# Joining each weight piece one step later in a fused scan and gated feed-forward kernel

## Chip, core and metric

The kernel runs on one core of a Trainium2 chip. Its time is the device time of one execution in microseconds (us); before the change the median of three executions is 376.66 us (376.62 to 376.97). The profiled execution spans 374.1 us, and the profile grants TensorE its full clock all through it.

Names used below, as in the profile: PE is TensorE (matrix products), PEld its loading of weights, DVE is VectorE, ACT is ScalarE, POOL is GpSimd, SP is SyncE, which here only issues transfers. L668 is line 668 of the kernel before. "hp", "k", "w", "gT", "mag" and so on are the names of tiles.

## What is computed

Two blocks follow each other. The first is a chunked state-space scan over x, a, B, C (4 sequences, 8 heads, 768 positions, 32 features, state 16). Its result, seen as a matrix of 3072 rows and 256 columns, goes through a feed-forward block:

```
h = x @ w_in          # 3072 x 256 by 256 x 2048
g = h * cos(h)
out = g @ w_out       # 3072 x 2048 by 2048 x 256
```

The two weight matrices arrive as 64-bit floating-point numbers, while the kernel calculates in 32 bits. So the kernel rebuilds each weight from its two 32-bit words before TensorE can use it. That rebuilding is what the change moves.

## The kernel before, in words

**Tiling.** The sequence is cut into six chunks of 128 positions, and all four sequences of a chunk are done together (512 rows). Each chunk needs 16 feed-forward steps, so step n belongs to chunk n // 16, and there are 96 steps. In chunk 0 two neighbouring steps, 2i and 2i+1, use the same pair i of 128-column blocks of w_in and the matching two row blocks of w_out: step 2i for one half of the rows and step 2i+1 for the other. In the later chunks each half has its eight steps in a row.

**One step.** `first(n)` (L668) forms h on PE: eight matmuls of 128x256 in a PSUM tile hp. `wind_k(n)` (L675, ACT) rounds h over 2 pi to an integer k, `wind_w(n)` (L681, DVE) subtracts it, `gate(n)` (L690, ACT) takes the cosine by a sine, and `gated(n)` (L695, DVE) multiplies it with h and leaves gT in SBUF. `second(n)` adds the product with w_out two steps later (LAG is 2): L739 in chunk 0, L777 after it. The hp tiles of ordinary steps come from two PSUM banks in turn, so `first(n+2)` can start only when `gated(n)` has read its bank.

**Order.** The schedule is manual: every engine does its instructions in the order in which the program emits them. In the main loop PE is given `first(n)`, then `second(n-2)`, and then, at some steps, the products of the scan. DVE is given `wind_w(n)`, the join of a weight piece if the step has one, `gated(n)`, and then what the list `behind` holds: halves of the decay scan of the next chunk (`halved`, a DVE scan over arow at L515) and masked products (`masked`, L586).

**Weight pieces.** w_in and w_out are cut into eight pieces each, named ("in", 0) to ("in", 7) and ("out", 0) to ("out", 7). Piece i of either serves steps 2i and 2i+1 of chunk 0. Each is fetched as 128 x 512 pairs of words. Two stages rebuild it:

- `grade`: ACT takes the absolute value of the high word as a float (L231, to mag), POOL clips it (L232), and ACT converts the low word (L229, to last). With `later=True` the last of these is emitted separately, behind `gate`.
- `join`: DVE shifts the bits (L244) and puts in the sign and top bits from the high word (L246); POOL adds the low bits and writes the finished piece into w_in or w_out (L254).

The table `piece` names a piece for each step of chunk 0: ("out", n/2) for an even n and ("in", (n+3)/2) for an odd one. The loop at step n grades `piece[n + 1]` and joins `piece[n]`. The steps 0 to 3 are written out by hand in `first_steps`, which also grades and joins ("in", 3) and grades ("out", 2); the main loop begins at step 4 (AHEAD). Tiles mag and last have three buffers each, words has eight.

**Later users of the engines.** From step 14 on POOL forms sums and differences of w_out blocks (`differ_w`, L714), and from step 16 on those of gT (`differ`, L720 to L723), for the seven-product scheme (`seven`) that the later chunks use.

Of the kernel before, what the change touches and what calls it, by code (L numbers as in the profile page):

```python
# [25 lines left out]
def kernel(  # L26
# [168 lines left out]
    def kept(which, i):  # L195
        return (w_in[:, :, i * WC:(i + 1) * WC] if which == "in" else
                w_out[:, i * WF:(i + 1) * WF])
# [12 lines left out]
    held = {}  # L210

    def shares(which, ap, n):

        return [ap] if n == 1 else [ap.rearrange("p (k e f) -> p e k f", k=KT, e=n)[:, e]
                                    for e in range(n)]

    def grade(which, i, later=False, n=1):


        t = words.pop((which, i), None)  # L220
        if t is None:
            return
        mag = conv.tile([P, 2 * WC], FP32, tag="mag", bufs=3, name="mag")
        last = conv.tile([P, 2 * WC], U32, tag="last", bufs=3, name="last")
        low, high, mags, lasts = (shares(which, ap, n) for ap in (t[:, :, 0], t[:, :, 1], mag, last))
        held[which, i] = list(zip(high, shares(which, mag.bitcast(U32), n), lasts))

        def rest(e=0):
            ACT.activation(lasts[e], low[e], AF.Copy, scale=2.0 ** -29)  # L229
        for e in range(n):  # L230
            ACT.activation(mags[e], high[e].bitcast(FP32), AF.Abs)  # L231
            G.tensor_scalar(out=mags[e], in0=mags[e], scalar1=MOST, scalar2=LEAST,  # L232
                            op0=ALU.min, op1=ALU.max)
            if not later:
                rest(e)
        if later:
            return rest

    def join(which, i):


        parts = held.pop((which, i), ())
        for e, (high, bits, last) in enumerate(parts):
            V.tensor_scalar(out=bits, in0=bits, scalar1=3, scalar2=0x3FFFFFFF,  # L244
                            op0=ALU.logical_shift_left, op1=ALU.bitwise_and)
            V.scalar_tensor_tensor(out=bits, in0=high, scalar=0xC0000000, in1=bits,  # L246
                                   op0=ALU.bitwise_and, op1=ALU.bitwise_or)
            dst = kept(which, i)
            if len(parts) > 1:
                dst = dst[:, :, e * P:(e + 1) * P]  # L250
            else:
                bits, last = (ap.rearrange("p (k f) -> p k f", k=dst.shape[1])
                              for ap in (bits, last))
            G.tensor_tensor(out=dst.bitcast(U32), in0=bits, in1=last, op=ALU.add)  # L254
# [10 lines left out]
    for s in range(2):  # L265
# [3 lines left out]
        out=a_in, in_=a.rearrange("(u b) h (c p) -> (b h c) u p", u=NU, p=P))  # L269
# [96 lines left out]
    def weigh0(k):  # L366
        scs[k] = sc = scan.tile([P, 2 * H, N], FP32, tag="sc0", bufs=1, name="sc0")
        G.tensor_tensor(out=sc, in0=bs[:, k].rearrange("p q (h n) -> p (q h) n", h=H),
                        in1=lams[k].rearrange("p q h i -> p (q h) i")[:, :, W - 1:W]
                        .to_broadcast([P, 2 * H, N]), op=ALU.mult)  # L370
# [53 lines left out]
    def weights(k, q):  # L424

        m_of[k] = units[k]
        m, l = (ap[:, :, HH * q:HH * (q + 1)].rearrange("p s (k t) i -> p k s (t i)", k=2)
                for ap in (units[k], lams[k]))
        V.tensor_tensor(out=m, in0=gs[k, q][:, :, 0:2 * P].rearrange("p k (s i) -> p k s i", s=2),
                        in1=l, op=ALU.mult)  # L430
# [224 lines left out]
    def first(n, between=None, tag="h"):  # L655
        c, f = divmod(n, NF)
        hp[n] = bank([P, TB], "hp", tag) if tag else pair("hp")[:, 0]

        u, j = turn_of(n)
        if c == 0:  # L660
            to_, y = hp[n].rearrange("p (e i) -> p e i", e=2), yT[0][:, u]
        else:
            to_ = hp[n].rearrange("p (e t s i) -> p e t s i", e=2, t=2, s=2)
            y = yT[c].rearrange("p k (u s t i) -> p k u t s i", u=2, s=2, t=2)[:, :, u]
        for e in range(2):
            fs = slice((2 * j + e) * P, (2 * j + e + 1) * P)
            for k in range(KT):
                PE.matmul(to_[:, e], lhsT=w_in[:, k, fs], rhs=y[:, k],  # L668
                          start=(k == 0), stop=(k == KT - 1), skip_group_check=True)
            if between and e == 0:  # L670
                between()

    def wind_k(n):
        k = ffn.tile([P, TB], I32, tag="k", name="k")
        ACT.activation(k, hp[n], AF.Copy, bias=0.25, scale=INV_2PI)  # L675
        turns[n] = k
# [11 lines left out]
    def gate(n):  # L688
        cos = turns[n]
        ACT.activation(cos, cos, AF.Sin, bias=quarter, scale=TWO_PI)  # L690
# [181 lines left out]
    def units_of_decay():  # L872
        G.tensor_copy(out=unit[:, 0:HH * P].rearrange("p (h i) -> p h i", h=HH),
                      in_=ident.unsqueeze(1).to_broadcast([P, HH, P]))
        G.tensor_copy(out=unit[:, HH * P:], in_=ident[:, 0:W])
# [10 lines left out]
    piece = {n: ("in", (n + 3) // 2) if n % 2 else ("out", n // 2) for n in range(NF)}  # L886
# [47 lines left out]
    def first_steps():  # L934

        grade("in", 1)
        weigh0(1)
        units_of_decay()
        for q in range(2):
            weights(1, q)  # L940
        states_of = []
        first(0, lambda: states_of.extend(finish0(1)))
        take_s1, add_s1 = states_of
        join("in", 1)
        rests = [grade("out", 0, later=True)]
        wind_k(0)
        take_s1()
        rests.pop()()
        wind_w(0)
        first(1)  # L950
        join("out", 0)
        wind_k(1)
        gate(0)
        wind_w(1)
        gate(1)
        gated(0)
        gated(1)
        first(2, tag=None)
        rests = [grade("in", 2, later=True)]
        clips()  # L960
        wind_k(2)
        rests.append(grade("out", 1, later=True))
        rests.pop(0)()
        wind_w(2)
        join("in", 2)
        first(3, tag=None)
        gate(2)
        rests.pop()()
        join("out", 1)
        gated(2)  # L970
        second(0)
        wind(3)
        rest = grade("in", 3, later=True)
        gate(3)
        rest()
        second(1)
        join("in", 3)
        gated(3)
        grade("out", 2)
        return add_s1  # L980

    add_s1 = first_steps()
# [1 line left out]
    for n in range(AHEAD, NC * NF + LAG):  # L984
        c, f = divmod(n, NF)
        if n < NC * NF:

            if c > 0 and f == (NJ if c == 1 else 0):
                if c == 1:
                    load(2, only=(x,))  # L990
                load(c + 2)
            first(n)
            wind(n)
            for at in pairs(n):
                turn2(*at)
            rests = []
            if n + 1 in piece:
                rests.append(grade(*piece[n + 1], later=True))
            gate(n)
            for rest in rests:  # L1000
                if rest:
                    rest()
            if n in piece:
                join(*piece[n])

            behind = [lambda at=at: halved(*at) for at in halves_at(n)]
            behind = [lambda at=(c, 2 * u + 1): masked(*at) for c, u in pairs(n - 2)] + behind
            if n not in piece and behind:
                behind.pop(0)()
            gated(n)  # L1010
            if n == AHEAD + 2:
                add_s1()
            for do in (*behind, *unsummed):
                do()
            unsummed.clear()
        for i, js in differ_at.get(n, ()):
            differ_w(i, js)
        if n >= LAG:
            second(n - LAG)
        for c, u in pairs(n - 1):  # L1020
            intra2(c, u)
            masked(c, 2 * u)
        for c, us in ends(n):
            finish2(c, us)
            if 1 in us:
                raw.pop(c)
        for c, u in pairs(n + 1):
            for b in (2 * u, 2 * u + 1):
                reaches(c, b)
                load_along(c + 1, (b,))  # L1030
            if by_blocks(c, u):
                turn_blocks(c, u)
        for at, (c, u) in block_loads.items():
            if at == n:
                loading = load_blocks(c, u)
            if at <= n < at + 8:
                for _ in range(4):
                    next(loading)
# [30 lines left out]
```

## Time and profile before

| engine | busy, us | share of the span | instructions |
|---|---|---|---|
| PE | 364.3 | 97% | 3262 |
| DVE | 282.7 | 76% | 473 |
| POOL | 216.1 | 58% | 334 |
| ACT | 172.1 | 46% | 293 |

The shares are averages over stages. Chunk 0's steps of the main loop lie between about 27 and 80 us; there DVE is much busier than its average. A busy share of PE is not PE at its peak, because its matmuls overlap and their ends are modelled, so PE is best judged by its idle times and by the distance between the starts of neighbouring groups. The mean durations of the operations that the change moves, where nothing disturbs them: L231 0.67 us, L229 0.67 us (ACT), L232 0.61 us (POOL), L244 0.42 us and L246 0.69 us (DVE), L254 1.27 us (POOL). One half of the decay scan (L515, 128 x 512) takes 1.92 us in this stage.

### The profile page before, as it was taken

How to read it: one execution, taken by the hardware profiler on the slowest of the kernel's cores; microseconds unless marked ns; L12 is line 12 of the kernel's file. 1: busy time of each engine (PE TensorE's matmuls, PEld its weight loads, DVE VectorE, ACT ScalarE, POOL GpSimd, SP SyncE). 2: the span in 40 equal slices, each digit the busy share in tenths (PEclk: the TensorE clock that was granted, in tenths of full speed). 3: DMA queues.
4: the chain of work that ended last, by engine and by line, in shares of the span. 5: the costliest groups of instructions: out<-in, count | busy, mean ns of one | idle time of the engine just before them, and what ended most of it. 6: DMA issues, size and time to landing. Idle time of an engine off the chain costs nothing.

```text
span 374.1 us, 8667 instructions
## 1 busy us (share of the span) xinstructions
PE 364.3 (97%) x3262; PEld 326.9 (87%) x3262; DVE 282.7 (76%) x473; ACT 172.1 (46%) x293; POOL 216.1 (58%) x334
## 2 busy tenths in 40 slices
PE   8998999999999999999999999999999999999996
PEld 5687777889899899999899998999999989999995
DVE  7788999989699957987867987766887872554543
ACT  3586756444344434354434435434444443443442
POOL 6667765589946346665454693453785344544451
PEclk9999999999999999999999999999999999999999
DMA  9969797514545742653222745221020000010011
GB/s 147 283 180 257 206 255 127 128 14 97 140 106 76 133 95 31 88 151 93 59 54 22 133 99 135 28 45 17 3 41 8 13 18 2 2 28 0 2 31 29
DMA packets 121354, 31.55 MB, mean 84 GB/s; under 512 B 90496, under 2 KB 117216, under 8 KB 121312
## 3 DMA queue, kind: packets, MB, share of 16 engines
q1 hardware_dynamic: 119024, 30.54, 38.3%
q10 hardware_dynamic: 2288, 0.46, 0.7%
q8 instruction: 26, 0.43, 0.5%
q14 instruction: 16, 0.13, 0.1%
HBM read 27.64 MB, written 3.34 MB: 83 GB/s over the span
## 4 chain that ended last, share of the span: by engine, by line
PE 64%; DVE 13%; SPq 7%; POOL 7%; issue 4%; ACT 2%; DMA 2%; DVEq 0%; POOLq 0%; ACTq 0%
PE hp L668 30%; PE o L777 25%; SPq L155 4%; POOL words L714 3%; DVE gT L695 2%; DVE w L681 2%; PE y L607 2%; SPq L110 2%; DVE mag L246 2%; DVE lam L515 2%; DVE mag L244 2%; DMA arow<-a_cut 1%; PE y L600 1%; PE g L565 1%; PE a_ps L351 1%
## 5 line engine op out<-in xcount | busy, mean ns | idle before, releaser
L668 PE MATMUL hp<-yT,w_in 128*128 128x256 f32 x768 | 183.5, 382 | 3.2 <-DVE gT L695 2.9
L668 PEld LDWEIGHTS hp<-yT,w_in 128*128 128x128 f32 x768 | 139.3, 190 | 23.8 <-issue 5.7
L720 POOL TENSOR_TENSOR gd<-gT 128x256 f32<-128x256 f32 x79 | 59.0, 747 | 99.1 <-DVE gT L695 97.2
L690 ACT ACTIVATE w<-w,quarter 128x512 f32<-128x512 f32 x96 | 69.2, 721 | 80.2 <-DVE w L681 80.1
L681 DVE SCALAR_TENSOR_TENSOR w<-hp,k 128x512 f32<-128x512 f32 x96 | 65.5, 682 | 40.4 <-ACT k L675 40.2
L675 ACT ACTIVATE k<-hp 128x512 int32<-128x512 f32 x96 | 57.1, 595 | 79.7 <-PE hp L668 79.5
L695 DVE TENSOR_TENSOR gT<-hp,w 128x512 f32<-128x512 f32 x96 | 65.2, 680 | 33.2 <-ACT w L690 24.3
L777 PE MATMUL o<-words,gd 128*128 128x128 f32 x474 | 65.9, 275 | 0.0
L777 PEld LDWEIGHTS o<-words,gd 128*128 128x128 f32 x474 | 59.3, 192 | 0.0
L515 DVE TENSOR_TENSOR_SCAN lam<-arow,unit 128x512 f32<-128x512 f32 x40 | 56.5, 1411 | 0.0
L777 PEld LDWEIGHTS o<-w_out,gT 128*128 128x128 f32 x316 | 47.6, 191 | 3.9
L723 POOL TENSOR_TENSOR gd<-gT,gd 128x128 f32<-128x128 f32 x79 | 44.6, 565 | 6.2
L777 PE MATMUL o<-w_out,gT 128*128 128x128 f32 x316 | 48.0, 275 | 0.0
L722 POOL TENSOR_TENSOR gd<-gT,gd 128x128 f32<-128x128 f32 x79 | 44.1, 558 | 6.2
L586 DVE TENSOR_TENSOR m<-g,lam 128x256 f32<-128x256 f32 x80 | 30.9, 414 | 0.5
L739 PE MATMUL o<-w_out,gT 128*128 128x256 f32 x128 | 30.2, 380 | 0.4 <-POOL w_out L254 0.4
L777 PE MATMUL o<-w_out,gd 128*128 128x128 f32 x158 | 30.6, 275 | 0.0
L777 PE MATMUL o<-words,gT 128*128 128x128 f32 x158 | 30.6, 275 | 0.0
L739 PEld LDWEIGHTS o<-w_out,gT 128*128 128x128 f32 x128 | 24.2, 190 | 4.0 <-POOL w_out L254 0.8
L777 PEld LDWEIGHTS o<-words,gT 128*128 128x128 f32 x158 | 24.0, 192 | 0.0
L777 PEld LDWEIGHTS o<-w_out,gd 128*128 128x128 f32 x158 | 24.0, 192 | 0.0
L794 DVE TENSOR_TENSOR sum<-ps,sum 128x256 f32<-128x256 f32 (+1 forms) x27 | 16.7, 644 | 0.6
(109 smaller groups left out, 269.5 us busy)
## 6 DMA issues: line engine op xcount, KB each, us to landing
arow<-a_cut SPq DMA_DIRECT2D x20, 512.0 KB
words<-in_moe_w_in_dram SPq DMA_DIRECT2D x8, 512.0 KB
words<-in_moe_w_out_dram SPq DMA_DIRECT2D x8, 512.0 KB
out_dram<-sum SPq DMA_DIRECT2D x18, 128.0 KB
blocks<-in_B_dram SPq DMA_DIRECT2D x128, 8.0 KB
blocks<-in_C_dram SPq DMA_DIRECT2D x128, 8.0 KB
xr<-in_x_dram SPq DMA_DIRECT2D x14, 128.0 KB
along<-a_all SPq DMA_DIRECT2D x20, 64.0 KB
```

Source lines behind the costliest of these rows:

```text
L515: V.tensor_tensor_scan(out=lam[c, b][:, hs].rearrange("p h i -> p (h i)"), data0=rows_.rearrange("p h i -> p (h i)"), data1=unit[:, b % 2 ...
L586: V.tensor_tensor(out=m_[js, :, :, is_], in0=g_[js, :, :, is_], in1=l_[js, :, :, is_], op=ALU.mult)
L668: PE.matmul(to_[:, e], lhsT=w_in[:, k, fs], rhs=y[:, k], start=(k == 0), stop=(k == KT - 1), skip_group_check=True)
L675: ACT.activation(k, hp[n], AF.Copy, bias=0.25, scale=INV_2PI)
L681: V.scalar_tensor_tensor(out=w, in0=hp[n], scalar=INV_2PI, in1=k, op0=ALU.mult, op1=ALU.subtract)
L690: ACT.activation(cos, cos, AF.Sin, bias=quarter, scale=TWO_PI)
L695: V.tensor_tensor(out=gT[n], in0=hp.pop(n), in1=cos, op=ALU.mult)
L720: G.tensor_tensor(out=d[:, 0:2], in0=g[:, 1:2].to_broadcast([P, 2, P]), in1=g[:, 3::-3], op=ALU.subtract)
L722: G.tensor_tensor(out=d[:, 2], in0=g[:, 0], in1=d[:, 0], op=ALU.subtract)
L723: G.tensor_tensor(out=d[:, 3], in0=g[:, 2], in1=d[:, 2], op=ALU.subtract)
L739: PE.matmul(o[c, u][:, t], lhsT=g[:, 2 * e + t], rhs=w_out[:, 2 * j + e], start=(j == e == t == 0), stop=(j == NJ - 1 and e == 1), skip_gr ...
L777: PE.matmul(at[q], lhsT=a_[q], rhs=w[q], start=(j == 0 and q in starts), stop=(j == NJ - 1), skip_group_check=True)
```

## The change

Until now the piece that is joined at step n was graded at step n-1. The new loop grades `piece[n]` at step n and joins `piece[n - 1]`. So the distance between grading and joining stays one step, and both move one step later, for the pieces ("in", 3) and ("out", 2) and all after them. Step 3 loses its join, which moves to step 4, and the grading of ("out", 2) moves from the end of `first_steps` to step 4. A step that joins nothing may run the first entry of `behind` between wind_w and gated; before, all sixteen steps of chunk 0 were excluded from this, since they all have an entry in `piece`, and now step 14, which joins nothing, is not. The purpose is to keep Abs, clip and join away from one another in time, and to fill the DVE's gap between w and gT with a scan.

```diff
@@ first_steps
         second(1)
-        join("in", 3)
         gated(3)
-        grade("out", 2)
         return add_s1
@@ main loop
-            rests = []
-            if n + 1 in piece:
-                rests.append(grade(*piece[n + 1], later=True))
+            rest = grade(*piece[n], later=True) if n in piece else None
             gate(n)
-            for rest in rests:
-                if rest:
-                    rest()
-            if n in piece:
-                join(*piece[n])
+            if rest:
+                rest()
+            joins = n - 1 in piece and piece[n - 1] in held
+            if joins:
+                join(*piece[n - 1])
...
-            if n not in piece and behind:
+            if not joins and behind:
                 behind.pop(0)()
             gated(n)
```

The instructions of every engine stay the same in number and size. The order changes on DVE, ACT and POOL; PE's order is the same.

## The prediction

> **What bounds the kernel now.** I read the page first, then the busy times by stage, then who waited for whom between 20 and 80 us, then the order of time on three engines there.
>
> ```profile
> PE 364.3 (97%) x3262; PEld 326.9 (87%) x3262; DVE 282.7 (76%) x473; ACT 172.1 (46%) x293; POOL 216.1 (58%) x334
> ```
>
> PE sets the end: once it is late, nothing later makes that up, unless PE idles later. The table by stage (length, then busy us of PE, PEld, DVE, ACT, POOL) shows that only the stage of the edit leaves PE room:
>
> ```profile
> 20.00:40.00 20.00, 18.30 (x81) 14.90 (x81) 16.55 (x24) 14.36 (x25) 13.16 (x15) 1.00 0.73 186
> 40.00:60.00 20.00, 19.12 (x89) 15.95 (x88) 19.83 (x25) 13.09 (x24) 14.68 (x16) 1.00 0.85 224
> 60.00:80.00 20.00, 20.00 (x176) 16.94 (x175) 17.84 (x32) 9.63 (x17) 11.23 (x12) 1.00 0.53 107
> ```
>
> DVE, with 19.83 of 20 us, is the bound from 40 to 60 us. The waits of 20 to 80 us (total, times, longest) say how that reaches PE:
>
> ```profile
> PE hp L668 <- DVE gT L695: 1.9, 5, 0.6
> PE o L739 <- POOL w_out L254: 0.4, 1, 0.4
> DVE mag L244 <- POOL mag L232: 2.1, 3, 1.0
> DVE w L681 <- ACT k L675: 1.2, 4, 0.4
> ```
>
> PE waits for gT, that is for its PSUM bank. It waits for a finished w_out piece only once, at step 2. The order of time on PE, DVE and POOL around steps 5 to 8:
>
> ```profile
> 35.64 1.96 PE L668 MATMUL hp<-yT,w_in 128*128 128x256 f32 x8 [0.61 <-DVE gT L695]
> 37.44 1.89 PE L739 MATMUL o<-w_out,gT 128*128 128x256 f32 x8
> 39.72 1.97 PE L668 MATMUL hp<-yT,w_in 128*128 128x256 f32 x8 [0.39 <-DVE gT L695]
> 41.52 1.89 PE L739 MATMUL o<-w_out,gT 128*128 128x256 f32 x8
> 43.25 1.89 PE L668 MATMUL hp<-yT,w_in 128*128 128x256 f32 x8
> 44.98 1.89 PE L739 MATMUL o<-w_out,gT 128*128 128x256 f32 x8
> ```
> ```profile
> 35.41 1.92 DVE L515 TENSOR_TENSOR_SCAN lam<-arow,unit 128x512 f32<-128x512 f32 x1
> 37.26 0.66 DVE L681 SCALAR_TENSOR_TENSOR w<-hp,k 128x512 f32<-128x512 f32 x1
> 37.84 0.41 DVE L244 TENSOR_SCALAR mag<-mag 128x512 uint32<-128x512 uint32 x1
> 38.28 0.69 DVE L246 SCALAR_TENSOR_TENSOR mag<-words,mag 128x512 uint32<-128x512 uint32 x1
> 38.89 0.68 DVE L695 TENSOR_TENSOR gT<-hp,w 128x512 f32<-128x512 f32 x1
> ```
> ```profile
> 34.98 1.27 POOL L254 TENSOR_TENSOR w_out<-mag,last 128x512 uint32<-128x512 uint32 x1 [1.09 <-DVE mag L246]
> 39.06 1.28 POOL L254 TENSOR_TENSOR w_in<-mag,last 128x512 uint32<-128x512 uint32 x1 [1.32 <-DVE mag L246]
> ```
>
> The L668 rows are first(6), first(7), first(8), the L739 rows second(4) to second(6). Back to back a group takes 1.73 us, a step 3.46, two steps 6.92. Piece out 2 is ready at 34.98 + 1.27 = 36.25, and second(4) starts at 37.44: slack 1.2 us. From the same rows at later steps the slack of out 3, 4, 5, 6, 7 is 1.8, 1.3, 1.2, 2.8 and 4.2 us.
>
> **What the Trainium skill says.** "SBUF — State Buffer", section "Who interferes with whom": a DVE tensor_scalar may enter a two-port mode and then competes with GpSimd for one pair of ports, where the second to issue waits for the whole of the first. The trace agrees: L244 takes 0.42 us alone, but 1.48 at 25.91 us, beside a POOL L254 of 25.84 to 27.11. "Perfetto Trace Analysis", section "DVE / Act Engine Instruction": the profiled time of an instruction omits the wait for semaphores and their spreading. Here the hop between engines shows as a gap, 0.03 to 0.16 us, so below I use distances between starts.
>
> **The change part by part.**
>
> *Work.* No instruction is added or removed. Eleven joins leave their step for the next. DVE time is the same in sum, 0.42 + 0.69 us a join.
>
> *Gain at step 3.* DVE waits there 0.83 us for the clip of in 3 and spends 1.07 on the join before gated(3), which starts at 31.22; ACT does Abs and last of out 2 (1.16 us) ahead of k(4), at 31.71. Without these, k(4) follows last(in 3) at 30.55, w(4) is at 30.55 + 0.63 = 31.18, in 3 is joined (L244 31.78, L246 32.23), and gated(4) starts at 32.84 instead of 34.81. DVE is 2.0 us ahead. For PE this is worth 0.76 us: first(6) may start as soon as second(3) has ended, 34.88 instead of 35.64. in 3 is ready for it at 32.23 + 0.78 + 1.32 = 34.33. The other w_in pieces keep a step or more of slack: their edit costs nothing, hidden behind second(n) and first(n+1).
>
> *The new wait.* out i is now joined at step 2i+1, on DVE behind gated(2i), a scan at steps 4 and 8, and w(2i+1). PE needs it straight after first(2i+2), so it queues in front of first(2i+3), whose h feeds k, w and gT. In the profile before, the L254 of that next step (or w plus the same distances where it had none) plus 1.32 comes after the start of second(2i) by 2.9, 3.5, 2.9, 2.8, 0.8 and 0.6 us for out 2 to 7. The 2.0 us of lead, and PE's own lateness, pay part of it. The rest I get by stepping on:
>
> Distances: first to k 1.98, k to w 0.63, w to L244 0.60, L244 to L246 0.45, L246 to L254 0.78, L254 to second 1.32: 5.76 us from first(2i+1) to second(2i), and 1.80 more to first(2i+3), which restarts. So two steps can't take less than 7.56 us, even if DVE is never late. PE alone would need 6.92; before, first(7) to first(9) took 7.32 and first(9) to first(11) 7.47.
>
> - Step 5: gated(4) 32.84, scan to 35.28, w 35.28, L246 36.33, L254 37.11, second(4) 38.43, first(7) 40.26, against 39.72: +0.5.
> - Step 7: k 42.32, w 42.95, L246 44.0; POOL is held until 44.9 by the state update (1.68 + 0.87), a weighting (0.86) and a clip, second(6) 46.25, first(9) 48.05 against 47.04: +1.0.
> - Step 9: w 50.68, L254 52.51, second(8) 53.83, first(11) 55.63 against 54.51: +1.1.
> - Step 11: two reach scans and a small product ahead, L246 59.75, L254 60.53, second(10) 61.85, first(13) 64.5 (with 0.83 of scan products) against 63.48: +1.0.
> - Step 13: had no join before; second(12) 70.25, first(15) 73.9 (with 1.83 of scan products) against 72.42: +1.5.
> - Step 15: the same; second(14) 79.65, first(17) 81.45 against 79.43: +2.0.
>
> *The scan at step 14* goes before gated(14): gated ends at 74.1, and first(16) comes at 77.3. It costs nothing, hidden behind first(15) and second(13).
>
> *Unknown sizes.* (a) Now k paces DVE, so L244 falls due at k + 1.23 and the clip L232 at k + 1.25, on the same ports. L244 took 0.85 beside an L232 at 56.70. That is 0 to 0.43 us on the chain at each of five steps, 0 to 2.1; I take 0.6. (b) The first scan now comes at 33.44. Its arow was issued at 28.33; another took 4.34 us from issue, so 32.7 at best, and the scan of before puts it at 35.41 at worst: 0 to 2.0, I take 0.4. (c) PE idles 1.3 us after 80 us, waiting for gT and POOL, which may absorb 0 to 1.0; I take 0.3. POOL's L714 work waits behind the later scan, so I don't take more.
>
> Sum: 2.0 + 0.6 + 0.4 - 0.3 = +2.7 us, 379.4 us.
>
> **Rivals.**
> - *Even exchange*: the wait for w_out replaces the wait for gT, 7.56 a pair against 7.3 to 7.5, and POOL and the scans are kinder than assumed. For it: the two loops differ by only 0.1 to 0.2 us a pair. Against it: from 64 us on PE had no idle time to exchange. About +0.5 us, 377.2.
> - *Faster*: DVE's 2.0 us of lead survives, and the 1.9 us of gT waits go without new ones; second(2i) never waits. -1.9 us, 374.8. For it: DVE is the bound to 60 us. Against it: slack of 1.2 to 1.8 us can't cover a shift of a whole step.
> - *Heavier*: collisions and the late arow at their upper ends: 2.0 + 2.1 + 2.0 - 0.3, less what overlaps, about +5, 381.7. For it: L244 and L246 were stretched before in half of the steps. Against it: DVE has then idle time that takes some of it up.
>
> **How the numbers follow.** Forecast 0.60 (378.2 to 381), even exchange 0.13, faster 0.14, heavier 0.13. Low end 376.8 leaves out the faster case; high end 381.8 leaves out half of the heavier one. Slower by over 0.2% (0.75 us): 0.60 + 0.13 and a third of the exchange, 0.77; faster 0.14; within 0.2% 0.09.
>
> **What would show it.** Right: PE L739 waits for POOL w_out L254 at four or more even steps, 0.5 to 2 us each, 4 us or more together; the waits of L668 for gT nearly vanish; DVE shows idle time before w, waiting for k; first(17) starts 2 to 3 us later. Step 3: gated(4) near 32.8. Wrong: L254 of out pieces ends before second(2i) wants it, or arow or POOL hold DVE instead, or PE's lateness at 80 us is gone by the end.

## The result and the profile after

The changed kernel takes 381.72 us (median of 11 executions, 380.05 to 384.17) against 377.46 us for the kernel before on the same chips: a ratio of 1.0101, with a 95% interval of 1.0074 to 1.0129 (the two medians alone would give 1.0113). On 376.66 us that is 3.8 us slower, 2.8 to 4.9. The spread of the eleven goes with the mean granted clock: five executions at 0.999 to 1.0 took 380.05 to 381.18 us, six at 0.996 took 381.72 to 384.17. The profiled execution, at full clock, spans 378.9 us instead of 374.1. The work is the same; PE's share went down:

```profile
PE 365.3 (96%) x3262; PEld 327.2 (86%) x3262; DVE 283.6 (75%) x473; ACT 172.6 (46%) x293; POOL 216.7 (57%) x334
```

By stage (length, then busy us of PE, PEld, DVE, ACT, POOL), in the changed kernel:

```profile
20.00:40.00 20.00, 17.37 (x79) 14.33 (x78) 16.37 (x25) 14.68 (x26) 12.98 (x14) 1.00 0.75 207
40.00:60.00 20.00, 18.39 (x86) 15.56 (x85) 18.12 (x24) 11.47 (x21) 13.01 (x14) 1.00 0.83 223
60.00:80.00 20.00, 18.37 (x166) 14.84 (x165) 15.78 (x29) 9.92 (x17) 10.75 (x11) 1.00 0.54 111
```

PE lost 0.93, 0.73 and 1.63 us of busy time in the three stages, and DVE, which was full from 40 to 60 us (19.83), now has room there. So DVE is no longer the full engine of that stage, and PE is idle more than before. The waits between 20 and 84 us in the changed kernel say for what (three of the list; total, times, longest):

```profile
PE o L739 <- POOL w_out L254: 6.1, 7, 1.9
DVE w L681 <- ACT k L675: 5.8, 8, 1.8
DVE mag L244 <- POOL mag L232: 1.0, 1, 1.0
```

The five waits of L668 for gT (1.9 us) are gone. In their place PE waits at every second(2i) for the w_out piece. DVE's idle time is now in front of w, waiting for k, that is for PE. So each waits for the other in turn: PE for the piece that DVE and POOL join, DVE for the k that ACT makes of PE's h. The order of time on PE, from first(6) to first(9):

```profile
35.15 1.89 PE L668 MATMUL hp<-yT,w_in 128*128 128x256 f32 x8
38.98 1.99 PE L739 MATMUL o<-w_out,gT 128*128 128x256 f32 x8 [1.94 <-POOL w_out L254]
40.81 1.89 PE L668 MATMUL hp<-yT,w_in 128*128 128x256 f32 x8
42.53 1.89 PE L739 MATMUL o<-w_out,gT 128*128 128x256 f32 x8
44.26 1.89 PE L668 MATMUL hp<-yT,w_in 128*128 128x256 f32 x8
47.04 1.99 PE L739 MATMUL o<-w_out,gT 128*128 128x256 f32 x8 [0.89 <-POOL w_out L254]
48.88 1.89 PE L668 MATMUL hp<-yT,w_in 128*128 128x256 f32 x8
```

The six new waits, at second(4), (6), (8), (10), (12) and (14), are 1.94, 0.89, 0.72, 1.11, 0.52 and 0.49 us: 5.67 together (the seventh of the list, 0.43 us at second(2), was there before). A group after a wait takes 1.83 us to the next one instead of 1.73, so the six cost 0.6 more. Less the 1.88 us of the old gT waits and 0.07 us of restart at each of their five, that is 4.0 us. first(17) starts at 83.92 instead of 79.43, 4.5 us later, of which 0.3 was there before the change had any effect (first(4) starts at 27.45 instead of 27.16). Little is added afterwards: the end is 4.8 us later. These 4.8 us are of one pair of executions; the ratio, of many, gives 3.8.

The chain that ended last, between 60 and 69 us of the changed kernel, shows the loop of the prediction (start, us, engine; lines left out at "..."):

```profile
60.91 0.34 DVE mag L244
61.28 0.99 DVE mag L246
...
62.34 1.28 POOL w_out L254
...
63.67 1.99 PE o L739 x8
65.66 0.81 PE g L565 x24
66.47 1.97 PE hp L668 x8
...
68.52 0.61 ACT k L675
...
69.75 0.43 DVE mag L244
```

Before, the chain in this stretch never went through L254 to L739. Here the joined piece releases second(10), which stands in front of first(13), whose h gives k, and k the next join.

### The profile page after: what moved, and what is told of

Same layout as the page of the kernel before. It is cut to its first block, busy times and chain, and to the rows that moved or that the text cites. A ratio compares the mean times of both kernels' runs of the same rounds, so it can differ in the third digit from the quotient of the medians.

```text
span 378.9 us, 8664 instructions
## 1 busy us (share of the span) xinstructions
PE 365.3 (96%) x3262; PEld 327.2 (86%) x3262; DVE 283.6 (75%) x473; ACT 172.6 (46%) x293; POOL 216.7 (57%) x334
## 4 chain that ended last, share of the span: by engine, by line
PE 77%; DVE 7%; SPq 5%; POOL 3%; issue 2%; DMA 2%; ACT 2%; DVEq 0%; POOLq 0%; ACTq 0%
PE hp L668 36%; PE o L777 30%; SPq L110 4%; PE y L607 3%; PE o L739 2%; PE g L565 2%; DMA words<-in_moe_w_out_dram 1%; PE y L600 1%; DVE mag L246 1%; DVE mag L244 1%; POOL w_out L254 1%; PE a_ps L351 1%; DVE w L681 1%; ACT k L675 1%; PE warm L84 1%
## 5 line engine op out<-in xcount | busy, mean ns | idle before, releaser
L668 PE MATMUL hp<-yT,w_in 128*128 128x256 f32 x768 | 183.1, 382 | 1.1 <-DVE gT L695 0.6
L668 PEld LDWEIGHTS hp<-yT,w_in 128*128 128x128 f32 x768 | 139.6, 190 | 20.1 <-issue 2.4
L777 PE MATMUL o<-words,gd 128*128 128x128 f32 x474 | 65.8, 275 | 0.0
L777 PEld LDWEIGHTS o<-words,gd 128*128 128x128 f32 x474 | 59.3, 192 | 0.0
L515 DVE TENSOR_TENSOR_SCAN lam<-arow,unit 128x512 f32<-128x512 f32 x40 | 57.5, 1437 | 0.6 <-DMA arow<-a_cut 0.6
L777 PEld LDWEIGHTS o<-w_out,gT 128*128 128x128 f32 x316 | 47.6, 191 | 4.0
L723 POOL TENSOR_TENSOR gd<-gT,gd 128x128 f32<-128x128 f32 x79 | 45.5, 577 | 6.2
L777 PE MATMUL o<-w_out,gT 128*128 128x128 f32 x316 | 48.0, 274 | 0.0
L722 POOL TENSOR_TENSOR gd<-gT,gd 128x128 f32<-128x128 f32 x79 | 44.2, 559 | 6.2
L739 PE MATMUL o<-w_out,gT 128*128 128x256 f32 x128 | 30.8, 385 | 6.1 <-POOL w_out L254 6.1
L739 PEld LDWEIGHTS o<-w_out,gT 128*128 128x128 f32 x128 | 23.7, 190 | 11.8 <-POOL w_out L254 8.9
L777 PE MATMUL o<-w_out,gd 128*128 128x128 f32 x158 | 30.5, 275 | 0.0
L777 PE MATMUL o<-words,gT 128*128 128x128 f32 x158 | 30.5, 275 | 0.0
L777 PEld LDWEIGHTS o<-w_out,gd 128*128 128x128 f32 x158 | 24.0, 192 | 0.0
L777 PEld LDWEIGHTS o<-words,gT 128*128 128x128 f32 x158 | 24.0, 192 | 0.0
L232 POOL TENSOR_SCALAR mag<-mag 128x512 f32<-128x512 f32 x16 | 12.6, 784 | 8.3 <-ACT mag L231 8.2
```

Source lines behind the costliest of these rows:

```text
L515: V.tensor_tensor_scan(out=lam[c, b][:, hs].rearrange("p h i -> p (h i)"), data0=rows_.rearrange("p h i -> p (h i)"), data1=unit[:, b % 2 ...
L668: PE.matmul(to_[:, e], lhsT=w_in[:, k, fs], rhs=y[:, k], start=(k == 0), stop=(k == KT - 1), skip_group_check=True)
L722: G.tensor_tensor(out=d[:, 2], in0=g[:, 0], in1=d[:, 0], op=ALU.subtract)
L723: G.tensor_tensor(out=d[:, 3], in0=g[:, 2], in1=d[:, 2], op=ALU.subtract)
L739: PE.matmul(o[c, u][:, t], lhsT=g[:, 2 * e + t], rhs=w_out[:, 2 * j + e], start=(j == e == t == 0), stop=(j == NJ - 1 and e == 1), skip_gr ...
L777: PE.matmul(at[q], lhsT=a_[q], rhs=w[q], start=(j == 0 and q in starts), stop=(j == NJ - 1), skip_group_check=True)
```

## Experiments

Each kernel below calculates the whole result and was timed beside the kernel before on the same chip. Ratios are to that kernel, with 95% intervals. The changed kernel itself is 1.0101 (1.0074 to 1.0129).

### Only the w_in pieces late

```diff
-        join("in", 3)
...
+    joined_at = {}
+    for n, w in piece.items():
+        joined_at.setdefault(n + (w[0] == "in"), []).append(w)
```

This and the next kernel start from the kernel before; the loop grades what the table names for step n+1 and joins what it names for step n.

> Only the w_in pieces move one step later; the w_out pieces are graded and joined at their old steps (so the even steps join two pieces, the odd ones none; same work). Theory (the loss is PE waiting for w_out pieces joined too late): no wait of PE L739 for POOL w_out L254 from step 4 on, gated(4) still early, first(17) within 1 us of the kernel before, time 376.5 to 378.5 us. Rival (joining any piece later, w_in too, costs through the lead and order on DVE): 380 us or more.

Measured: 383.84 us, ratio 1.0182 (1.0159 to 1.0204). The expectation failed, and the time is on the rival's side. gated(4) is not early either: it starts at 36.11. The wait for w_out from step 4 on is indeed gone, but PE waits more than ever for gT (20 to 84 us):

```profile
PE hp L668 <- DVE gT L695: 7.9, 8, 1.8
PE o L739 <- POOL w_out L254: 0.4, 1, 0.4
```

Steps 6 and 7 on DVE show why:

```profile
41.65 0.69 DVE L681 SCALAR_TENSOR_TENSOR w<-hp,k 128x512 f32<-128x512 f32 x1 [0.91 <-ACT k L675]
...
43.32 0.42 DVE L244 TENSOR_SCALAR mag<-mag 128x512 uint32<-128x512 uint32 x1
43.77 1.64 DVE L246 SCALAR_TENSOR_TENSOR mag<-words,mag 128x512 uint32<-128x512 uint32 x1
45.34 0.68 DVE L695 TENSOR_TENSOR gT<-hp,w 128x512 f32<-128x512 f32 x1
45.94 1.97 DVE L515 TENSOR_TENSOR_SCAN lam<-arow,unit 128x512 f32<-128x512 f32 x1
47.83 0.66 DVE L681 SCALAR_TENSOR_TENSOR w<-hp,k 128x512 f32<-128x512 f32 x1
49.28 0.69 DVE L695 TENSOR_TENSOR gT<-hp,w 128x512 f32<-128x512 f32 x1 [0.79 <-ACT w L690]
```

The second join of the even step takes 1.64 us for L246, because POOL is adding up the first piece (L254 from 43.55 to 44.86), and gT starts 3.69 us after w (41.65). In the odd step the gap between w and gT is empty, and DVE idles 0.79 us in it while ACT takes the cosine. So a join that lies alone in that gap is almost free (w to gT takes 1.63 us with it at step 5 of the kernel before, 1.46 without at step 13), and two in one gap are not. That is a cost of my regrouping. The changed kernel keeps one join a step, so this run says nothing for or against the cause of its loss, beyond that the w_out waits come from the w_out pieces.

### Only the w_out pieces late

```diff
+    joined_at = {}
+    for n, w in piece.items():
+        joined_at.setdefault(n + (w[0] == "out"), []).append(w)
```

> Only the w_out pieces move one step later; the w_in pieces stay (so the odd steps from 5 on join two pieces, the even ones none, and a clip never falls beside a bit operation of the same step; same work). Theory (late w_out pieces): the waits of PE L739 for L254 stay and grow, since step 3's lead is gone: 1 to 2.5 us at each of steps 6, 8, 10, 12, time 381 to 384 us. Rival (the clip colliding with the bit operations on DVE is the main cost of the change): without collisions the time is 378 us or less.

Measured: 382.18 us, ratio 1.0137 (1.0107 to 1.0166), as the theory had it in time. The waits at steps 6, 8, 10 and 12 are 1.80, 0.96, 0.48 and 2.36 us, the second and third of them smaller than expected; all of them from 20 to 90 us:

```profile
PE o L739 <- POOL w_out L254: 7.0, 7, 2.4
```

From step 4 on no clip falls on a bit operation here, and the loss is there all the same; so collisions with the clip are not needed for it. The double joins add their part as in the run before (the second L246 of a step takes 1.64 us again), so the size isn't that of the w_out pieces alone.

### Clip moved away from the bit operations

```diff
-            rest = grade(*piece[n], later=True) if n in piece else None
             gate(n)
-            if rest:
-                rest()
...
                 join(*piece[n - 1])
+            if n in piece:
+                grade(*piece[n])
```

> The changed kernel, but the Abs goes behind the gate on ACT and the clip behind the join's L254 on POOL, so that clip L232 and the bit operations L244 and L246 of a step no longer fall together. Same work. Theory (collisions are a minor term, 0.3 us at each of five or six steps): L246 back to 0.69 us, the chain from first(2i+1) to second(2i) back to 5.8 us, gain 1 to 2 us on the changed kernel, 379.5 to 380.5 us, still slower than before. Rival (collisions are the main cost): 378 us or less.

Measured: 380.27 us, ratio 1.0084 (1.0065 to 1.0103): not told apart from the changed kernel, whose interval overlaps, and clearly slower than before. The time lies in the expected range, but the gain of 1 to 2 us that was to explain it is not to be seen: the span is 378.9 us in both. The collisions are gone (L246 takes 0.69 us at all but one of these steps), yet the waits of L739 for L254 are 6.5 us in total, against 6.1. In these two traces the steps from second(6) to second(10) are together 0.3 us shorter, while second(4) comes 0.4 us later (the scan before it waits 0.93 us for arow and takes 1.55) and second(6) another 0.3: there the clip takes 1.52 us beside a scan and delays the state update, behind which L254 stands. DVE waits only 0.45 us more for the clip. Moving the clip moved the lost time.

### The w_out pieces needed one step later

The direct test takes away what makes PE wait: in chunk 0 second(n) comes three steps after first(n), with one more gT buffer, in the changed kernel. The first version postponed all of them:

```diff
-bufs=LAG + 1, name="gT"
+bufs=LAG + 2, name="gT"
...
-        second(0)
...
-        second(1)
+        second(0)
...
-        if n >= LAG:
-            second(n - LAG)
+        for m in range(n - 3, n - 1):
+            if (m < NF) == (m == n - 3):
+                second(m)
```

> The changed kernel, but in chunk 0 second(n) comes three steps after first(n) instead of two (one more gT buffer), so a w_out piece is needed one step later. Same work. Theory (late w_out pieces are the whole loss): the waits of PE L739 for L254 vanish, step 3's lead stays, and the time falls to the kernel before or below it, 374.5 to 376.7 us. Rival (DVE order or ports also cost): waits of L668 for gT come in their place and the time stays at 379 us or more.

Measured: 378.22 us, ratio 1.0031 (1.0009 to 1.0053), between the theory and its rival. The waits for w_out are gone, and two thirds of the loss with them, but not all; those for gT that the rival named are absent up to 84 us. PE waits 3.6 us for w_in pieces instead (20 to 84 us), 2.0 of them at first(4), which second(1) used to precede. The second version leaves second(0) and second(1) where they were:

```diff
+            if m > 1 and (m < NF) == (m == n - 3):
```

> The changed kernel; in chunk 0 second(n) for n from 2 on comes three steps after first(n), and second(0) and second(1) stay in front of first(4), where PE waits anyway (they moved in the first version of this experiment). Theory (waits of PE for w_out pieces are the loss): no such wait after step 3, and about 1.7 us less than with all of them postponed: 376 to 377.2 us, level with the kernel before. Rival (the later w_in pieces and the DVE order cost too): 378.2 us or more.

Measured: 378.17 us, ratio 1.0021 (1.0004 to 1.0037). PE's waits from 20 to 84 us are only these:

```profile
PE hp L668 <- POOL w_in L254: 2.8, 3, 2.0
```

So with the need for the w_out pieces moved, four fifths of the loss is gone (1.0101 to 1.0021). The expected 376 to 377.2 us was missed by 1 us, and the rival's 378.2 us nearly reached, with the kernel before at 377.44 in that session. Nor is the second version measurably better than the first. PE runs ahead to first(6) and waits 1.99 us there for the w_in piece ("in", 3), and at the change to chunk 1 it waits 0.73 us for the copy of an output bank: both come from the postponing. The control does the same to the kernel before:

> Control: the kernel before with the same postponed second(n), n from 2 on. Theory: it hardly ever waited for w_out pieces, and DVE paces first(n), so nothing is gained: within 1 us of the kernel before, 376 to 377.7 us, with the waits of L668 for gT still there. Rival (postponing helps any order of joins): 375 us or less.

Measured: 377.61 us, ratio 1.0008 (0.9988 to 1.0028): no change that can be told. There 3.0 us of waiting for gT at first(6) take the place of the w_in wait. With the postponing in both, the two orders of joins are level within their intervals. The traces say the same: second(16), the first L777, starts at 85.05 us in the kernel before and at 89.53 in the changed one, but with the postponing at 87.05 and 86.24. The loss of the change therefore hangs on when second(2i) needs its piece.

One thing disturbs these two traces. Shortly after the wait at first(6) the granted clock falls to 0.50 for about 3.4 us. In the changed kernel with the postponing:

```profile
34.73 2.99 PE L668 MATMUL hp<-yT,w_in 128*128 128x256 f32 x8 [1.99 <-POOL w_in L254]
37.51 2.62 PE L739 MATMUL o<-w_out,gT 128*128 128x256 f32 x8
39.97 1.89 PE L668 MATMUL hp<-yT,w_in 128*128 128x256 f32 x8
```

The two groups take 5.24 us instead of 3.5, in the control 5.21, so PE may meet fewer waits after them than at full clock. The times do not hang on it: executions with a mean clock of 0.998 or more have medians of 377.86 us (postponed change) and 377.63 (control), against 377.34 for the kernel before.

### The scan at step 14 put back

```diff
-            if not joins and behind:
+            if n not in piece and behind:
```

> The changed kernel without its second part: at step 14 the scan stays behind gated(14). Same work. Prediction's step (this part costs nothing, hidden behind first(15) and second(13)): same time as the changed kernel within 0.3 us, 380.3 to 382 us. Rival (the scan ahead of gated(14) delays PE): 380 us or less.

Measured: 380.64 us, ratio 1.0092 (1.007 to 1.0114); the span is 378.8 us against 378.9, and PE waits for L254 the same 6.1 us. The second part of the change neither costs nor brings anything that can be told.

### The same clip order in the kernel before

> The kernel before with Abs and clip emitted behind the join of the step, so that the clip L232 no longer falls on L244 and L246. DVE is the bound from 36 to 66 us there, and L244 and L246 lie some 3 us above their undisturbed 0.42 and 0.69 us in sum. If the collisions are what DVE loses, 375 to 376.3 us, with less waiting of L668 for gT; if the lost time only moves (to waits for L232 or to other pairs), 376.4 to 377.5 us.

Measured: 377.20 us, ratio 1.0004 (0.9984 to 1.0023), with 1.9 us of waiting for gT as ever. From step 4 on L244 and L246 are back to 0.41 to 0.56 and 0.69 to 0.77 us, but DVE waits 3.5 us for the clip instead of 2.1. The lost time moves here too.

### Postponing from second(4) to second(14) only

```diff
+            if m > 1 and (4 <= m < NF - 1) == (m == n - 3):
```

In the changed kernel, in the kernel before, and in the changed kernel with the clip moved:

> The changed kernel with only second(4) to second(14) three steps behind first; second(2) and second(3) at their old steps (so PE does not run into the unfinished third w_in piece at step 6), and second(15) two steps behind (so the copy of the output bank at step 18 is not waited for). Same work. Theory: the 1.99 us wait for a w_in piece and the 0.73 us wait for the bank of the run before are gone or halved, and the kernel is level with the kernel before or a little faster, 375.5 to 377 us. Rival (the postponing itself leaves PE as late): 377.8 us or more.

> The kernel before with the same. Theory: DVE paces it, 376.2 to 377.4 us, the waits for gT stay, and it is not faster than the changed kernel with it.

> The changed kernel with the same postponing and, besides, Abs and clip behind the join. If collisions of the clip with L244 and L246 still cost where PE no longer waits for w_out, 0.3 to 1 us less than without; if they only move, no difference.

Measured: 379.15 us, 1.0028 (1.0003 to 1.0053); 378.68 us, 1.0022 (0.9999 to 1.0046); 380.31 us, 1.0053 (1.0019 to 1.0087). The first two expected times were missed, the first on the rival's side; of the third's two cases it is the second, no gain from moving the clip. Nothing beats the kernel before, which took 377.63 us here. PE's waits in the first of them, over the whole rest of the run, from 20 to 374 us:

```profile
PE hp L668 <- DVE gT L695: 2.5, 3, 1.3
PE g L565 <- ACT cT L549: 1.7, 1, 1.7
PE hp L668 <- POOL w_in L254: 1.6, 3, 1.0
PE o L739 <- POOL w_out L254: 0.4, 1, 0.4
```

PE no longer waits for w_out pieces from step 4 on, but still for gT and for w_in pieces. The wait of 1.7 us for cT comes at 185 us, far behind the stage of the edit: it follows a block transfer at the end of a long row of issues on SP. The changed kernel with the clip moved has it too, with 1.8 us, so it is no accident of one execution. Why that row ends later here than in the kernel before, whose PE waits for no cT, was not settled.

## Why the prediction was right

*What bounds.* Right: DVE paced the stage from 40 to 60 us before, and PE could lose time there that nothing later gave back. The lateness of 4.5 us at first(17) became 4.8 us at the end. The 0.3 us that I took off as absorbed later was wrong in sign.

*Gain at step 3.* Right: gated(4) starts at 33.41, or 33.12 without the 0.3 us of earlier offset, against 32.84 forecast and 34.81 before. first(6) follows second(3) without a wait, as forecast.

*The new wait.* Right in place, cause and nearly in size. Forecast for second(4) to second(14) were 1.82, 0.80, 0.59, 0.60, 0.56 and 0.56 us (from the steps: second's start less the end of first before it), 4.93 in all; measured 5.67. (By the prediction's own distances k of step 7 falls at 42.24, not 42.32; POOL held the chain there, so nothing hangs on it.) That the lateness of the w_out pieces is the cause is shown by the postponing, which takes away 0.8 of the 1.0%, while the control neither gains nor loses anything that can be told.

*The scan at step 14 and the w_in pieces cost nothing.* Shown for the scan. For the w_in pieces the trace of the changed kernel has only the 0.3 us wait that was there before; the run that moved them alone was spoilt by double joins. But the reason given, "a step or more of slack", was wrong: ("in", 4) to ("in", 7) were ready 2.5, 2.1, 1.3 and 3.3 us before their first(2i), a step being 3.46. PE, late by its waits for w_out, hid this. Where the postponing takes those away, PE waits 2.8 us for w_in pieces in the changed order and 0.3 in the order before.

*Where the size was off.* Forecast +2.7 us, measured about +3.8 by the ratio: inside the forecast's band of 378.2 to 381 us, but the 2.7 lies just under the measured interval. In the pair of traces first(17) is 2.2 us behind my step times, after the offset is taken off, where I had added 1.0 for (a) and (b). Two terms were too small. The first is (a), the collisions, taken as 0.6 us of a range of 0 to 2.1. They struck L246 too, which I had priced undisturbed: 0.98 instead of 0.69 us at steps 9 and 11 and at most of the even ones, and L244 took 0.85 at step 10:

```profile
52.55 0.98 DVE L246 SCALAR_TENSOR_TENSOR mag<-words,mag 128x512 uint32<-128x512 uint32 x1
...
56.47 0.85 DVE L244 TENSOR_SCALAR mag<-mag 128x512 uint32<-128x512 uint32 x1
...
61.28 0.98 DVE L246 SCALAR_TENSOR_TENSOR mag<-words,mag 128x512 uint32<-128x512 uint32 x1
```

DVE has no gap between the first and the last of these, so the three add up, to 1.0 us; by first(13) PE was 1.6 us behind my times. At step 7 the clip took 1.05 us behind the state update and held L254 by about 0.45. The second is the distance of 5.76 us from first(2i+1) to second(2i): at steps 13 and 15, without any collision, it was 5.96 and 5.93, mostly because k came 2.09 us after a first that follows scan products, instead of 1.98. Term (b) was about right, in part by luck: the scan waited 0.59 us for arow, but then took 1.25 us instead of 1.92, so that w(5) came 0.3 us late. Term (c) had the wrong sign, as said. That removing the collisions by moving the clip brought no measurable time does not contradict this: in that run the time was lost in other places.

*Rivals.* The even exchange failed because the new waits are three times the old ones; the faster case because a shift of a whole step exceeds slack of 1.2 to 1.8 us, as argued against it. The heavier case, about +5 us, lies just above the measured interval. It was right that collisions would weigh more, but not about arow, whose lateness did not come near its upper end.

## What to carry to other kernels

Ask of each conversion that is moved later how long before its consumer it was ready, and compare that slack with the distance of the move: here 1.2 to 1.8 us against a step of 3.5. Then count the whole way from the input of the step to the consumer over all engines; when it closes a loop with the bound engine (5.76 us forecast to second, 5.93 to 6.90 measured from step 7 on, and 1.80 more to the next first, against 6.92 of work), idle time on DVE doesn't help. In this kernel the gap that ACT's cosine opens on DVE held one join almost free, and two not.

## What was unexpected of the hardware

The bit operation L246, with two inputs in SBUF, took 0.69 us alone, 0.98 beside the clip on POOL, and 1.64 where it started just after a POOL addition of 1.31 us. The scan L515 of 128x512 took 1.21 to 1.25 us where no POOL instruction was under way when it started, and 1.91 to 1.98 where it started about 0.4 us after a POOL addition (L254) of 1.27. In the other order it was POOL that lost: a clip that started 0.21 us behind a scan of 1.25 us took 1.46 instead of 0.61. A group of PE matmuls behind a wait took 1.80 us (for gT) or 1.83 (for a weight piece) to the next, against 1.73 back to back.
